# One load of a two-stage kernel (state-space scan, then gated feed-forward) moved from the head of block 1 to its middle

**Chip, cores, metric.** One core of a Trainium2 chip. The metric is device microseconds of one execution, lower is better; a profiled execution also gives its span (first to last instruction), some 1.8 us shorter than the time.

## The reference, cut to what matters

```python
# 4 sequences x 8 heads x 768 positions, 32 wide, state 16, float32
for each chunk of positions, in order:
    y      = (C B^T * decay mask) x  +  decayed (C state)
    state  = decay * state + decayed (B^T x)
# then, over 3072 tokens of 256 numbers (y with heads joined):
h   = y @ w_in            # 256 -> 2048
out = (h * cos(h)) @ w_out  # 2048 -> 256
```

## The kernel before

The kernel takes six chunks of 128 positions. Its main loop has 96 steps n, 16 to a block; block c = n // 16 runs the feed-forward of chunk c while the scan of chunk c + 1 is woven in. A step has a first matmul (`hp`), an activation over ScalarE, VectorE and ScalarE again (`k`, `w`, cos in place, `gT`) and, two steps later, a second matmul (`o`). All loads below are issued by one engine, SyncE (`nc.sync`), in program order. A chunk's B, C and x lie in one of two sets of buffers, so chunk 3 takes chunk 1's. From the second half of chunk 2 on, B and C for the transposed path come as 32 small "block" loads of 8 KB each, four to a step. The row loads (`arow`, 512 KB) and along loads (`along`, 64 KB) bring the decay factors of the scan.

```python
loads = ctx.enter_context(tc.tile_pool(name="loads", bufs=2))
...
def load(c, seqs=(0, NB)):                     # chunk c: B, (C,) x into tiles bc and xr
    ...
        raw[c] = (loads.tile([P, 2, NB * H, N], FP32, tag="bc", name="bc"),
                  loads.tile([P, NB, H, D], FP32, tag="xr", name="xr"))
    ...
    for dst, src in ((bc[:, 0, rs], B), (bc[:, 1, rs], C), (xr[:, rs], x))[::2 if c > 2 else 1]:
        nc.sync.dma_start(out=dst, in_=src[...])
...
def load_blocks(c, u):                         # 32 loads of [32, 4, 16] each
    ...
                    nc.sync.dma_start(out=to_[:, k, s, m, h], in_=of[m, h])
                    yield
...
def turn_blocks(c, u): ...                     # VectorE transposes: turned <- blocks
def turn2(c, u): ...                           # ScalarE: cT <- turned;  VectorE: rT
def intra2(c, u): ...                          # TensorE: g = cT x turned
def finish2(c, us): ...                        # TensorE: y, and s_ps, the last reader of x
...
halves_of = {2: [(2, 0, 0), (3, 0, 1), (5, 1, 0), (6, 1, 1), (7, 2, 0), (8, 2, 1), (10, 3, 0),
                 (11, 3, 1)]}                  # step in the block, sequence, half: VectorE's scans
...
block_loads = {NF * (c - 1) - 9 + 8 * u: (c, u) for c in range(2, NC) for u in range(2)
               if by_blocks(c, u)}             # chunk 2, half 1: steps 15 to 22

rest_of_loads()
for n in range(NC * NF + LAG):
    c, f = divmod(n, NF)                       # NF = 16
    if n < NC * NF:
        if f == 0 and c > 0:
            load(c + 2)
        first(n)
    ...
    # chunk 1's second half: finish2 at step 21
    # chunk 2's second half: turn_blocks at the end of step 26, turn2 in step 27, intra2 in step 28
    for at, (c, u) in block_loads.items():
        ...
            for _ in range(4):
                next(loading)
```

## Time and profile before

| | kernel before |
|---|---|
| time, median of its three runs | 383.96 us (383.78 to 384.23) |
| span of the profiled execution | 381.8 us |
| TensorE busy | 371.9 us, 97% |
| granted TensorE clock, mean | 0.989 |
| step 24 to step 40 (hp start to hp start) | 65.51 us |
| step 40 to step 56 | 58.74 us |

TensorE sets the time, so a pause of another engine costs only where TensorE runs out of work. The two last rows are the way to find such a place in a loop: equal pieces of work should take equal time. They, the hole between them and the chain of waits that leads to it are shown line by line in the prediction. In a line of a timeline the first number is the start, the second the time until the end of the group, and the bracket gives the idle time just before it and what ended that. A line with `<-` between two engines, such as `SPq L119 <- PE s_ps L509: 13.8, 1, 13.8`, is a wait: total us, times, longest. PE is TensorE, PEld its weight loads, DVE VectorE, ACT ScalarE, POOL GpSimd and SPq the queue of SyncE. The granted clock is the share of full speed that TensorE was given; "half clock" is 0.5.

### The profile page before, as it was taken

The page shows a single profiled execution, that of the slowest core. Times are in us where ns is not written, and L with a number is a line of the kernel's source. Part 1 is how long each engine was busy: PE and PEld are TensorE (multiplying, and loading weights), DVE is VectorE, ACT ScalarE, POOL GpSimd, SP SyncE. Part 2 cuts the span into 40 slices and gives each one's busy share as a digit, 9 for nine tenths or more (in the row PEclk, how much of TensorE's full clock was granted, in tenths as well). Part 3 has the DMA queues.
Part 4 walks back from the last instruction along what each step waited for, and adds up shares of the span by engine and source line. Part 5 has one row for each costly group of instructions (what it writes and reads, how often), then busy time and mean ns, then how long its engine had stood idle before and what let it go on. Part 6 is the DMA issues. An engine that isn't in the chain of part 4 may idle for free.

```text
span 381.8 us, 7915 instructions
## 1 busy us (share of the span) xinstructions
PE 371.9 (97%) x2952; PEld 328.6 (86%) x2952; DVE 278.5 (73%) x436; ACT 176.2 (46%) x305; POOL 213.7 (56%) x330
## 2 busy tenths in 40 slices
PE   8999999999999599999999999999999999999996
PEld 2578888888999499998989998989998989999995
DVE  8879999799687546987766887865888772554543
ACT  3887756444343233444433444443444443434441
POOL 6767564579764344694353775354666443444551
PEclk9999999999999699999999999999999999999999
DMA  6989889923544442944215843121020010010011
GB/s 81 258 230 290 250 218 131 164 59 29 78 112 98 106 107 21 136 116 114 46 22 61 146 96 80 22 39 18 4 40 8 2 27 2 2 28 2 2 27 27
DMA packets 123606, 31.48 MB, mean 82 GB/s; under 512 B 92753, under 2 KB 119473, under 8 KB 123569
## 3 DMA queue, kind: packets, MB, share of 16 engines
q1 hardware_dynamic: 123408, 30.86, 40.1%
q8 instruction: 23, 0.38, 0.4%
q10 hardware_dynamic: 160, 0.13, 0.1%
q14 instruction: 15, 0.11, 0.1%
HBM read 27.64 MB, written 3.34 MB: 81 GB/s over the span
## 4 chain that ended last, share of the span: by engine, by line
PE 93%; DVE 3%; POOL 1%; SPq 1%; DMA 1%; issue 1%; ACT 0%; DVEq 0%; POOLq 0%; ACTq 0%
PE hp L550 42%; PE o L647 31%; PE o L609 7%; PE g L454 3%; PE y L488 3%; PE y L481 1%; PE warm L101 1%; PE a_ps L317 1%; DVE mag L227 1%; PE g L392 1%; POOL w_in L235 1%; DMA blocks<-in_C_dram 1%; PE o L692 0%; PE s_ps L509 0%; DVE sum L664 0%
## 5 line engine op out<-in xcount | busy, mean ns | idle before, releaser
L550 PE MATMUL hp<-yT,w_in 128*128 128x256 f32 x768 | 185.5, 385 | 0.5 <-POOL w_in L235 0.3
L550 PEld LDWEIGHTS hp<-yT,w_in 128*128 128x128 f32 x768 | 140.5, 192 | 22.1 <-issue 3.5
L591 POOL TENSOR_TENSOR gd<-gT 128x256 f32<-128x256 f32 x79 | 59.9, 758 | 102.2 <-DVE gT L566 84.0
L561 ACT ACTIVATE w<-w,quarter 128x512 f32<-128x512 f32 x96 | 69.2, 721 | 73.6 <-DVE w L556 73.6
L556 DVE SCALAR_TENSOR_TENSOR w<-hp,k 128x512 f32<-128x512 f32 x96 | 65.5, 682 | 48.5 <-ACT k L554 48.2
L554 ACT ACTIVATE k<-hp 128x512 int32<-128x512 f32 x96 | 57.2, 595 | 89.3 <-PE hp L550 89.1
L566 DVE TENSOR_TENSOR gT<-hp,w 128x512 f32<-128x512 f32 x96 | 65.1, 678 | 34.3 <-ACT w L561 29.1
L647 PE MATMUL o<-words,gd 128*128 128x128 f32 x474 | 65.9, 275 | 0.0
L647 PEld LDWEIGHTS o<-words,gd 128*128 128x128 f32 x474 | 59.3, 192 | 0.0
L363 DVE TENSOR_TENSOR_SCAN lam<-arow,unit 128x512 f32<-128x512 f32 x40 | 55.8, 1395 | 0.0
L647 PEld LDWEIGHTS o<-w_out,gT 128*128 128x128 f32 x316 | 47.6, 191 | 4.1
L594 POOL TENSOR_TENSOR gd<-gT,gd 128x128 f32<-128x128 f32 x79 | 47.2, 598 | 6.2
L647 PE MATMUL o<-w_out,gT 128*128 128x128 f32 x316 | 48.0, 274 | 0.0
L593 POOL TENSOR_TENSOR gd<-gT,gd 128x128 f32<-128x128 f32 x79 | 42.4, 537 | 6.2
L609 PE MATMUL o<-w_out,gT 128*128 128x256 f32 x128 | 30.3, 380 | 0.4 <-POOL w_out L235 0.4
L647 PE MATMUL o<-words,gT 128*128 128x128 f32 x158 | 30.6, 275 | 0.0
L647 PE MATMUL o<-w_out,gd 128*128 128x128 f32 x158 | 30.5, 275 | 0.0
L609 PEld LDWEIGHTS o<-w_out,gT 128*128 128x128 f32 x128 | 24.2, 190 | 4.0 <-POOL w_out L235 0.8
L467 DVE TENSOR_TENSOR m<-g,lam 128x512 f32<-128x512 f32 x40 | 25.5, 679 | 0.0
L647 PEld LDWEIGHTS o<-words,gT 128*128 128x128 f32 x158 | 24.0, 192 | 0.0
L647 PEld LDWEIGHTS o<-w_out,gd 128*128 128x128 f32 x158 | 24.0, 192 | 0.0
L346 POOL TENSOR_TENSOR sc<-bc,lam 128x128 f32<-128x128 f32 x20 | 8.3, 417 | 16.7 <-DVE lam L363 9.4
(96 smaller groups left out, 286.0 us busy)
## 6 DMA issues: line engine op xcount, KB each, us to landing
arow<-a_cut SPq DMA_DIRECT2D x20, 512.0 KB
words<-in_moe_w_in_dram SPq DMA_DIRECT2D x8, 512.0 KB
words<-in_moe_w_out_dram SPq DMA_DIRECT2D x8, 512.0 KB
out_dram<-sum SPq DMA_DIRECT2D x18, 128.0 KB
xr<-in_x_dram SPq DMA_DIRECT2D x4, 512.0 KB
blocks<-in_B_dram SPq DMA_DIRECT2D x112, 8.0 KB
blocks<-in_C_dram SPq DMA_DIRECT2D x112, 8.0 KB
along<-a_all SPq DMA_DIRECT2D x20, 64.0 KB
```

The costliest lines, as they stand in the source:

```text
L363: V.tensor_tensor_scan(out=lam[c, b][:, hs].rearrange("p h i -> p (h i)"), data0=rows_.rearrange("p h i -> p (h i)"), data1=unit.rearrange ...
L467: V.tensor_tensor(out=of[0], in0=g[q][:, :, s * 2 * P:(s + 1) * 2 * P], in1=of[1], op=ALU.mult)
L550: PE.matmul(to_[:, e], lhsT=w_in[:, k, fs], rhs=y[:, k, u], start=(k == 0), stop=(k == KT - 1), skip_group_check=True)
L554: ACT.activation(k, hp[n], AF.Copy, bias=0.25, scale=INV_2PI)
L556: V.scalar_tensor_tensor(out=w, in0=hp[n], scalar=INV_2PI, in1=k, op0=ALU.mult, op1=ALU.subtract)
L561: ACT.activation(cos, cos, AF.Sin, bias=quarter, scale=TWO_PI)
L566: V.tensor_tensor(out=gT[n], in0=hp.pop(n), in1=cos, op=ALU.mult)
L591: G.tensor_tensor(out=d[:, 0:2], in0=g[:, 1:2].to_broadcast([P, 2, P]), in1=g[:, 3::-3], op=ALU.subtract)
L593: G.tensor_tensor(out=d[:, 2], in0=g[:, 0], in1=d[:, 0], op=ALU.subtract)
L594: G.tensor_tensor(out=d[:, 3], in0=g[:, 2], in1=d[:, 2], op=ALU.subtract)
L609: PE.matmul(o[c, u][:, t], lhsT=g[:, 2 * e + t], rhs=w_out[:, 2 * j + e], start=(j == e == t == 0), stop=(j == NJ - 1 and e == 1), skip_gr ...
L647: PE.matmul(at[q], lhsT=a_[q], rhs=w[q], start=(j == 0 and q in starts), stop=(j == NJ - 1), skip_group_check=True)
```

## The change

The intent: chunk 3's B and x are asked for at step 16, though B's buffer comes free only after chunk 1's transposes at step 18 and x's only after chunk 1's last matmuls at step 21, and SyncE stands waiting meanwhile. Asked for at step 24, they find the buffers free.

```diff
         if n < NC * NF:
-            if f == 0 and c > 0:
+
+            if c > 0 and f == (NJ if c == 1 else 0):     # NJ = 8
                 load(c + 2)
             first(n)
```

## The prediction

> **What bounds the kernel now.** I read the page's head and its slices first, then a table of stretches, then the SyncE queue's own waits, then each engine around the one place where TensorE stands still. The loop runs over 96 steps n; block c holds steps 16c to 16c+15. A step is one first matmul (hp), one second (o, two steps behind) and the activation between them; the state-space scan of the next chunk is woven in.
>
> ```profile
> span 381.8 us, 7915 instructions
> PE 371.9 (97%) x2952; PEld 328.6 (86%) x2952; DVE 278.5 (73%) x436; ACT 176.2 (46%) x305; POOL 213.7 (56%) x330
> PE   8999999999999599999999999999999999999996
> PEclk9999999999999699999999999999999999999999
> ```
>
> TensorE is busy 97% and sets the time. In the loop there is one hole: slice 14 (124 to 134 us), where both its busy share and its granted clock drop. The next view cuts the span at hp starts that the chain of waits gives: 107.06 is step 24, 172.57 step 40, 231.31 step 56. The three rows are therefore 16 steps each, from the middle of one block to the middle of the next.
>
> ```profile
> core 0: us, PE busy (x) PEld busy (x) DVE busy (x) ACT busy (x) POOL busy (x), PEclk, DMA share, GB/s
> 107.06:172.57 65.51, 61.49 (x513) 55.83 (x513) 47.35 (x73) 24.10 (x40) 35.28 (x56) 0.95 0.53 104
> 172.57:231.31 58.74, 58.74 (x514) 54.10 (x513) 44.03 (x71) 25.29 (x42) 33.04 (x55) 1.00 0.43 75
> 231.31:290.05 58.74, 58.74 (x514) 54.10 (x513) 43.89 (x71) 25.29 (x42) 31.89 (x51) 1.00 0.18 33
> ```
>
> The matmul counts are the same within one record, the later two rows are 58.74 us and full, the first is 65.51. So 65.51 - 58.74 = 6.77 us is all that this stretch can give back. A finer table of the hole shows its two halves:
>
> ```profile
> 121.50:124.80 3.30, 3.28 (x22) 2.88 (x21) 1.51 (x5) 0.00 (x0) 0.38 (x1) 1.00 0.58 162
> 124.80:128.80 4.00, 0.00 (x1) 0.00 (x1) 1.45 (x4) 0.96 (x3) 0.00 (x0) 0.84 0.28 50
> 128.80:130.90 2.10, 2.10 (x17) 1.30 (x17) 2.10 (x3) 1.04 (x2) 0.75 (x2) 0.50 0.71 195
> 130.90:134.55 3.65, 3.65 (x10) 2.94 (x11) 2.00 (x4) 0.72 (x1) 2.93 (x6) 0.52 0.30 52
> ```
>
> TensorE stands for 4.0 us and then works for 5.75 us at half clock. What it waits for, from the timelines of the engines and of the queue:
>
> ```profile
> 128.80 2.09 PE L454 MATMUL g<-cT,turned 32*128 32x256 f32 x16 [4.02 <-ACT cT L443]
> 127.84 0.91 ACT L443 ACTIVATE cT<-turned,slot 128x256 f32<-128x256 f32 x2 [7.22 <-DVE turned L423]
> 127.36 0.45 DVE L423 STREAM_TRANSPOSE turned<-blocks 128x256 f32<-128x256 f32 x1 [4.34 <-DMA blocks<-in_C_dram]
> 123.55 2.32 SPq L137 DMA_DIRECT2D blocks<-in_C_dram  x4
> ```
>
> The matmul g of step 28 needs cT, cT needs the transposed block, and the block needs the last of 32 small loads, which the queue issued only at about 125.3 us. Why so late is in the queue's own waits and its timeline:
>
> ```profile
> SPq L119 <- PE s_ps L509: 13.8, 1, 13.8
> 85.61 0.38 SPq L119 DMA_DIRECT2D bc<-in_B_dram  x1
> 99.90 0.37 SPq L119 DMA_DIRECT2D xr<-in_x_dram  x1
> 103.75 2.37 SPq L137 DMA_DIRECT2D blocks<-in_B_dram  x4
> ```
>
> Chunk 3's B and x are asked for at step 16, but their buffer is chunk 1's, and chunk 1's last reader (s_ps, step 21) ends at 99.84 us. The x load waits 13.8 us at the head of SyncE's queue, and 28 of the 32 block loads of chunk 2, second half, stand behind it.
>
> **What the Trainium skill says.** "Perfetto Trace Analysis", section on the DMA instruction (HWDGE), has an issuing sequencer go through its semaphore wait first and be free for its next instruction only after the descriptors are made. The trace agrees: between 86.0 and 99.9 us SyncE issues nothing. "DMA: Bandwidth & Descriptors", Anatomy of one DMA, gives some 2.0 us of fixed cost to a transfer; the chain of waits here has 2.00 us from the last block load's issue to the transpose. "TensorE: Matmul & The Clock Gate", What's actually happening, says the array falls to half rate after an idle window of about 3.4 us and comes back after about 3.4 us of work. The trace agrees on halving after a 4.0 us gap (16 g matmuls take 2.09 us against 1.08 elsewhere) but shows 5.75 us of slow work; I use the measured one.
>
> **The change, part by part.** *Removed:* the load at step 16. Nothing then waits at the head of the queue for s_ps. *Added:* the same two loads at step 24, after chunk 1's buffer was freed at step 21. The number of transfers, bytes and compute instructions is unchanged, and so is the order on every engine but SyncE's queue.
>
> *Where the block loads then go.* From 99.9 to 125.87 us the queue works without a break; less the x issue (0.37) that is 25.6 us of issuing, for the stores, rows and block loads of steps 16 to 22. Without the wait it starts on them when step 14's output copy is there, about 82.6 us (81.91 + 0.67). Unhindered it would end at 82.6 + 25.6 = 108.2 us. It also has to wait for scans that free row buffers: the one of step 17 ends at 84.3, of step 19 at 91.95, of step 22 at 104.3 us. From the last: a row load (0.42), two along loads (1.3), four block loads (2.3) give 108.3 us. So the last block is issued at about 108.3 and lands at about 110.3. VectorE reaches the second transpose at 122.97 (122.60 plus the 0.37 that one takes of a pair). Slack about 12.5 us: the wait is gone with much to spare.
>
> *What then binds step 28.* The same place one block later (step 44) is the pattern: two transposes take 0.74 us, cT starts 0.03 later and takes 0.91, g starts 0.31 after the last group of o. Here that gives transposes done at 122.60 + 0.74 = 123.34, cT done at 124.28; TensorE gets to g at 124.39 + 0.31 = 124.70. In time by 0.4 us. Next, hp of step 29 needs the bank that gT of step 27 reads. On VectorE: w starts 123.27, rT 123.84, the scan 124.17 (1.21 us; step 43 has no such scan), gT 125.29 to 125.95. TensorE is done with g at 124.70 + 1.08 = 125.78. So about 0.2 us is left waiting, too short for a clock drop by what the trace shows (1 us pauses are not there to compare, so this is my choice).
>
> *The sum.* Idle 4.02, g at half clock 2.09 - 1.08 = 1.01, hp at half clock 3.67 - 1.92 = 1.75: together 6.78, the 6.77 of the table by another way. Less the new wait of 0.2: 6.55 us. **383.96 - 6.55 = 377.4 us.** Elsewhere nothing can come: the chain from step 18 to 28 and from 40 on is matmul behind matmul.
>
> **The rivals.** *A. The wait moves to another transfer.* The two loads are now in front of step 24's rows and blocks. The x issue before took 0.37 us, others of that kind up to 3.6 us, and the store behind x took 2.63, so the queue may lose some 6 us after 111 us. But what stands behind them are chunk 3's second-half rows, its blocks (first transposed at step 38, about 160 us) and the first store of sum. Chunk 3's B is first read past step 32 (about 140 us), so the loads have 30 us. I give this 6%; it would leave 2 to 4 us of the gain unseen, 379.5 to 381.5.
>
> *B. VectorE becomes the bound at steps 26 to 29.* With 4.3 us of its own idleness gone it has a scan, four sums, two reach scans and two transposes in a row. It is busy 12.08 of 14.44 us from 107 to 121.5. If my offsets are off by 0.5 us, g or hp waits up to 1 us: 377.5 to 378.5. About 20%.
>
> *C. The gain is larger than the hole.* It would need TensorE time to be lost elsewhere through the same wait; the pieces of steps 18 to 28 are 3.29 us each plus g, y, tp, with no gap. Under 5%, and only noise would bring it past 2%.
>
> *D. The blocks come late anyway,* because the scans or 64-byte packets hold them. 512 KB rows and 64 KB along loads share the engines with them; but the slack is 12.5 us. 2%, time unchanged.
>
> **Range and chances.** Two per cent faster means at most 376.3 us, 7.7 less, and the hole is 6.8. So the change should fall just short of that mark: faster 0.05. Slower needs a new stall of over 14 us, for which I see no candidate: 0.01. Within 2%: 0.94. The low end of the range is the whole hole plus a little noise (0.2 us between runs), 376.8; the high end leaves 1 us to rival B: 378.4.
>
> **What would show it.** Right: no SyncE wait for s_ps; x of chunk 3 issued near 111 us without a wait; the last block load of chunk 2 issued near 108 us and no DMA named before turned; slice 14 at 9 for TensorE and for its clock; the stretch from step 24 to step 40 at 58.7 to 59.2 us; mean clock near 1.0 from the 0.989 before; g at 1.08 us after at most some tenths of idle. A wait of hp for gT of 0.1 to 0.4 us in step 29 would confirm the small term. Wrong: a TensorE gap over 1 us between 108 and 170 us, above all behind chunk 3's blocks, rows or B; or transposes waiting for a DMA with the queue's issues in time (then it was transfer, not order).

## The result, and the profile after

Beside 384.10 us of the kernel before (four runs, 383.78 to 384.41), the changed kernel took 377.96 us (four runs, 377.46 to 378.32). The ratio of the two is 0.9839, with a 95% interval of 0.9822 to 0.9856. A ratio is the mean time of one kernel's fast runs over that of the other's fast runs of the same rounds, so not quite the ratio of the medians quoted. The gain of 6.1 us is within the 2% that is called the same, as forecast.

The page of the kernel after, its head and two rows of its slices:

```profile
span 376.5 us, 7915 instructions
PE 369.5 (98%) x2952; PEld 327.0 (87%) x2952; DVE 278.4 (74%) x436; ACT 176.1 (47%) x305; POOL 213.7 (57%) x330
PE   8989999999999999999999999999999999999996
PEclk9999999999999999999999999999999999999999
```

The instruction counts are those of before. The 5 in TensorE's row and the 6 in the clock's row are gone.

Stretches of the kernel after, cut like those of before (108.26 is its step 24, 167.29 step 40, 226.03 step 56), and three short ones through the place where the hole was (columns as in the prediction):

```profile
108.26:167.29 59.03, 58.78 (x514) 54.11 (x513) 47.16 (x73) 24.11 (x40) 35.30 (x56) 1.00 0.58 95
167.29:226.03 58.74, 58.74 (x514) 54.11 (x513) 44.04 (x71) 25.29 (x42) 33.04 (x55) 1.00 0.41 73
...
125.99:127.06 1.07, 1.07 (x16) 0.64 (x16) 1.07 (x2) 0.58 (x2) 0.40 (x1) 1.00 0.62 152
127.06:127.31 0.25, 0.00 (x1) 0.03 (x1) 0.25 (x2) 0.00 (x0) 0.01 (x2) 1.00 0.07 18
127.31:129.27 1.96, 1.96 (x10) 1.75 (x11) 1.10 (x3) 0.72 (x1) 1.63 (x3) 1.00 0.22 45
```

The stretch came down from 65.51 to 59.03 us, a gain of 6.48 us. The pause of 4 us became one of 0.25 us, and g and hp run at full clock. SyncE's queue in the kernel after, from the timeline:

```profile
107.25 2.32 SPq L137 DMA_DIRECT2D blocks<-in_C_dram  x4
109.61 2.28 SPq L137 DMA_DIRECT2D blocks<-in_B_dram  x4
111.99 0.41 SPq L119 DMA_DIRECT2D bc<-in_B_dram  x1
112.50 2.69 SPq L119 DMA_DIRECT2D xr<-in_x_dram  x1
115.28 3.45 SPq L145 DMA_DIRECT2D arow<-a_cut  x1
```

Chunk 2's last four block loads start to be issued at 107.25 us (123.55 before), and only then come the next chunk's first blocks and the two moved loads, without a wait; the list of the queue's waits no longer has s_ps at all. What VectorE and TensorE do with the blocks:

```profile
123.80 0.74 DVE L423 STREAM_TRANSPOSE turned<-blocks 128x256 f32<-128x256 f32 x2
125.91 1.15 PE L454 MATMUL g<-cT,turned 32*128 32x256 f32 x16
127.31 1.96 PE L550 MATMUL hp<-yT,w_in 128*128 128x256 f32 x8 [0.25 <-DVE gT L566]
```

Both transposes run back to back, g starts without a bracket, and the 0.25 us before hp are the small new wait for gT.

**The span tells another sum.** It fell by 5.3 us only (381.8 to 376.5), 1.2 us less than the stretch gave. The missing part lies at the start, in code that the change does not touch. One hp and the first o matmul of the kernel before, then of the kernel after:

```profile
23.22 1.97 PE L550 MATMUL hp<-yT,w_in 128*128 128x256 f32 x8 [0.15 <-DVE gT L566]
25.61 1.99 PE L609 MATMUL o<-w_out,gT 128*128 128x256 f32 x8 [0.42 <-POOL w_out L235]
```

```profile
24.43 1.97 PE L550 MATMUL hp<-yT,w_in 128*128 128x256 f32 x8 [1.06 <-DVE gT L566]
26.82 1.99 PE L609 MATMUL o<-w_out,gT 128*128 128x256 f32 x8 [0.42 <-POOL w_out L235]
```

The profiled execution of the kernel after is 1.21 us late at 26.8 us already. Leave the start out: 381.8 - 25.61 = 356.19 us and 376.5 - 26.82 = 349.68 us, a gain of 6.51. Whether the late start belongs to the change is the first question below.

### The profile page after: what moved, and what is told of

It reads as the page before. It is cut to its first block, busy times and chain, and to the rows that moved or that the text cites. A ratio compares the mean times of both kernels' runs of the same rounds, so it can differ in the third digit from the quotient of the medians.

```text
span 376.5 us, 7915 instructions
## 1 busy us (share of the span) xinstructions
PE 369.5 (98%) x2952; PEld 327.0 (87%) x2952; DVE 278.4 (74%) x436; ACT 176.1 (47%) x305; POOL 213.7 (57%) x330
## 4 chain that ended last, share of the span: by engine, by line
PE 89%; SPq 4%; DMA 3%; DVE 2%; issue 1%; ACT 1%; POOL 0%; ACTq 0%; DVEq 0%; POOLq 0%
PE hp L550 42%; PE o L647 31%; PE o L609 7%; SPq L119 3%; PE g L454 3%; PE y L488 3%; DMA words<-in_moe_w_in_dram 2%; PE y L481 1%; DMA blocks<-in_B_dram 1%; PE o L692 1%; PE s_ps L509 0%; SPq L186 0%; DVE gT L566 0%; PE tp L437 0%; POOL w_out L235 0%
## 5 line engine op out<-in xcount | busy, mean ns | idle before, releaser
L664 DVE TENSOR_TENSOR sum<-ps,sum 128x256 f32<-128x256 f32 (+1 forms) x27 | 16.7, 644 | 0.6
```

## The experiments

Three accounts of the gain were open. **Queue order:** the x load waits for s_ps at the head of SyncE's queue, and the block loads behind it come late; the wait itself costs nothing. **Contention:** the 768 KB of B and x crowd the DMA engines just when the blocks are due, and it helps to have them out of the way. **The clock:** how much of the loss was idle time, and how much the half clock after it.

All results in one table. "Rest" is the span of the profiled execution less the start of its first o matmul, so free of the start; "stretch" is g of step 24 to g of step 40, sixteen steps. Times are medians; each ratio is against the kernel before on the same chip.

| run | time (runs) | ratio | first o | rest | stretch |
|---|---|---|---|---|---|
| kernel before | 383.96 (3) | 1 | 25.61 | 356.19 | 65.51 |
| kernel after | 377.96 (4) | 0.9839 | 26.82 | 349.68 | 59.03 |
| after_again | 377.41 (5) | 0.9823 | 25.90 | 349.70 | 59.04 |
| after_third | 377.50 (5) | 0.9826 | 26.57 | 349.73 | 59.04 |
| x_alone_late | 377.09 (4) | 0.9820 | 25.64 | 349.76 | 59.03 |
| b_alone_late | 384.43 (4) | 1.0001 | 26.05 | 356.45 | 65.77 |
| blocks_first | 378.03 (4) | 0.9833 | 26.40 | 349.70 | 59.03 |
| third_buffer | 378.10 (4) | 0.9848 | 26.59 | 349.71 | 59.02 |
| step18 | 377.14 (4) | 0.9831 | 25.59 | 349.71 | 59.04 |
| step17 | 382.57 (4) | 0.9945 | 26.91 | 354.39 | 63.74 |
| step17_again | 381.08 (4) | 0.9922 | 25.91 | 353.29 | 62.61 |
| row_first | 378.20 (4) | 0.9844 | 26.65 | 349.75 | 59.06 |
| filled_hole | 381.90 (4) | 0.9947 | 25.92 | 354.18 | 63.50 |
| scan_later | 377.29 (4) | 0.9828 | 26.19 | 349.41 | 58.77 |

The first o matmul started anywhere from 25.59 to 26.91 us, in kernels that do not differ before that point (third_buffer aside, which makes one table in place). The rest, by contrast, is the same within 0.1 us wherever the hole is closed (349.68 to 349.76), but for scan_later, which changes one thing more and has 349.41.

### The changed kernel twice more

The edit is none.

> The changed kernel once more, for its size and for the question why its first profile lay 1.2 us late before the hole was even reached. Theory (queue order): the stretch from step 24 to step 40 takes 59.0 us as in the first profile (65.51 before, 58.74 in steady state), time 377.5 to 378.2. If the late start (first o matmul at 26.82 us against 25.61) is scatter from run to run, it lies between 25.5 and 27 here, and differs from 26.82; if it belongs to the change, it is 26.8 again and again later than that of the kernel before.

> The changed kernel as the partner of the one with the later scan, on the same chip: stretch 59.0; first o matmul somewhere from 25.5 to 27 us, as the prologue falls out.

As expected: stretch 59.04 in both; the first o at 25.90 and 26.57 us in place of 26.82. So the late start is scatter from run to run, not a cost of the change. The medians, 377.41 and 377.50 us, are also a little under that of the first four runs.

### Which of the two loads counts

The edit, shortened (the code has slices for `B`, `x` and `both`):

```diff
+            # x_alone_late: B stays at step 16; b_alone_late: x stays there
-            if f == 0 and c > 0:
-                load(c + 2)
+            if f == 0 and c > 0:
+                load(c + 2, only=B if c == 1 else both)      # or: only=x
+            if c == 1 and f == NJ:
+                load(3, only=x)                              # or: only=B
```

> Only the x load is moved to step 24, B stays at step 16. Theory: x alone waits for s_ps (13.8 us), B waits only for the transposes of step 18 (3.5 us), so the whole gain comes from x: 377.5 to 378.3, stretch from step 24 to 40 at 59.0. Rival contention (it is the 768 KB out of the way of the block loads that helps, 256 KB of it B): part of the gain is missing, 379 to 381. Rival that both count: near 381.

> The counterpart: only B is moved, x stays at step 16 and waits for s_ps there. Theory: no gain, the hole is as before, 383.6 to 384.4, stretch from step 24 to 40 at 65 to 66 us and a SyncE wait for s_ps of some 14 to 17 us. Rival contention: a third of the bytes is gone from in front of the blocks, about 382.

x alone brings all of the gain and B alone none. The queue's waits with B alone moved, and the g matmul that follows from them:

```profile
SPq L120 <- PE s_ps L510: 18.1, 1, 18.1
...
129.44 2.09 PE L455 MATMUL g<-cT,turned 32*128 32x256 f32 x16 [4.22 <-ACT cT L444]
```

The wait for s_ps is even longer, 18.1 us in place of 13.8, since x now reaches the head of the queue without the B load's own wait before it; the hole stays as it was. With 256 KB out of the way of the blocks nothing was gained, which speaks against contention.

### The wait kept, but with nothing urgent behind it

```diff
-    block_loads = {NF * (c - 1) - 9 + 8 * u: (c, u) for ...
+    block_loads = {NF * (c - 1) - 9 + 8 * u - 8 * ((c, u) == (2, 1)): (c, u) for ...
```

> The load of B and x stays at step 16 as in the kernel before and still waits for s_ps, but the 32 block loads of chunk 2, second half, are put before it (steps 7 to 14 in place of 15 to 22). Theory: the wait is still there, 13 us or so, and costs nothing, because nothing that is due soon stands behind it: 377.5 to 378.3, stretch at 59.0. Rival (the wait itself costs, or what else stands behind it: stores, rows, along loads): a good part of the 6 us is still lost, 381 to 384.

The load is at step 16 as in the kernel before. The queue in this run, its waits and its timeline:

```profile
SPq L119 <- PE s_ps L509: 10.0, 1, 10.0
...
84.86 4.62 SPq L137 DMA_DIRECT2D blocks<-in_C_dram  x8
90.10 0.52 SPq L119 DMA_DIRECT2D bc<-in_B_dram  x1
100.69 0.37 SPq L119 DMA_DIRECT2D xr<-in_x_dram  x1
```

x waits for s_ps for 10 us (I had put down some 13), the stores, rows and along loads stand behind it, and the gain is there in full (rest 349.70). The wait itself costs nothing; the block loads behind it did.

### The early load kept, but without a wait

```diff
-                      loads.tile([P, NB, H, D], FP32, tag="xr", name="xr"))
+                      loads.tile([P, NB, H, D], FP32, tag="xr", name="xr", bufs=3))
-    la = const.tile([RB, NU, P], FP32, name="la")
+    la = a_in                                   # room for the third buffer
```

> The load stays at step 16, but x has three buffers, so chunk 3's x need not wait for chunk 1's (one small table is made in place to have the room; that is no work more or less). Theory: no wait for s_ps, blocks issued in time though B and x move at the old time among them: 377.5 to 378.3, stretch from step 24 to 40 at 59.0. Rival contention: 512 KB of x and 256 KB of B move just when the blocks do, blocks late, 380 to 384.

x in this run, from the queue's timeline:

```profile
87.01 2.09 SPq L119 DMA_DIRECT2D xr<-in_x_dram  x1
```

B is issued at 86.59 and x at 87.01 us, and stores and the block loads of steps 16 to 22 come right behind them. The rest is 349.71 us. So 768 KB in front of the blocks cost nothing once the queue doesn't wait: contention is refuted as the cause. The median of this run is at the slow end of the group; in its profiled execution the first o was late (26.59).

### How early may the load be?

```diff
-            if c > 0 and f == (NJ if c == 1 else 0):
+            if c > 0 and f == (1 if c == 1 else 0):      # step17; step18: 2
```

> The load of the change put at step 17 in place of 24: x still waits until 100 us or so, but the stores and four block loads of step 16 are in front of it. In the kernel before these took 3.33 and 2.37 us of queue time after x, some 2 us of it back-pressure of x that would fall on the next issue. Theory: the last block load is issued 3.5 to 5.7 us earlier than before, at 120 to 122.5, lands at 122 to 124.5, VectorE wants it at 123: g waits between 0 and 1.2 us, with no clock drop to speak of. 377.7 to 379.5, that is most of the gain for one step. Rival (any wait at the head of the queue costs its length): 383.

> The load at step 18, wait for s_ps still over 10 us. Theory: four more block loads, a row, two stores and two along loads are in front (5.4 us), so the last block lands by 120 and nothing waits for it: as the change, 377.5 to 378.3, stretch at 59.0, although the load waits at the head of the queue nearly as long. Rival: 382 to 383.

At step 18 the load waited 7.2 us for s_ps, less than the 10 us that I had put down, and nothing was lost. At step 17 my expectation failed: 382.57 us, with three runs at 382.2 to 383.1 and one at 379.33. The queue's timeline of step17 shows why the block loads gained so little:

```profile
101.20 0.37 SPq L119 DMA_DIRECT2D xr<-in_x_dram  x1
101.66 2.46 SPq L145 DMA_DIRECT2D arow<-a_cut  x1
104.21 2.98 SPq L617 DMA_DIRECT2D out_dram<-ob  x2
...
113.79 5.68 SPq L137 DMA_DIRECT2D blocks<-in_B_dram  x8
```

From x's issue at 101.20 to the last block load's end at 125.97 us the queue took 24.8 us, against 26.0 in the kernel before (99.90 to 125.87): 1.2 us won, where I had counted on 3.5 to 5.7. I had allowed for x holding up the next issue (2.46 us for a row load that takes 0.42 otherwise), but not for that row load, 512 KB itself, holding up the stores after it (2.98 us for two against 1.36). A further 1.05 us went to eight block loads (5.68 against 4.63). They stand 12 us later, behind another row load, as they do in the kernel before, so the first row load does not explain them; why they were slower was not tested. Two more runs were to test that.

```diff
+            # row_first: after the scan of step 17 and its row load, in place of before them
+            if n == NF + 1:
+                load(3)
```

> The load at step 17 once more, because my expectation of it missed by 4 us and its four times lay in two places (three near 382.7, one at 379.3). Reading of the first profile: x and the 512 KB of rows now follow one another in the queue, the DMA engines are full for 6 us behind them, and SyncE's later issues take longer (two stores 2.98 us against 1.36, eight block loads 5.68 against 4.63), so the last block was issued only 1.2 us earlier than before; at the edge, some executions still lose the clock. Expected: again times in both places or near 382.6, with the last block load issued at 124.5 to 126 us where it is slow and by some 123 where it is fast.

> The load at step 17 too, but behind that step's row load in place of in front of it. Reading (back-pressure of two large transfers in a row): what is left behind x takes 20.6 us of queue time by the durations of the kernel before (stores 3.33, along loads 1.30, blocks 4.63, row 0.42, blocks 4.63 and 2.28, row 0.42, along 1.25, blocks 2.32), so the last block is issued by about 121 after the x at 100.4 and lands at 123, the moment it is wanted: g waits at most some tenths, no clock drop, 377.2 to 378.5, stretch from step 24 to 40 at 59.0 to 59.6. Rival (step 17 was slow for a reason other than the order of rows and x): near 382.6 as before.

With the row load ahead of x, all is well: the last block load ends at 122.44 us, 21.5 us after x was issued, and g does not wait. So the order of x and that row load decides it, but the reason is shown only in part. The two stores, now right behind x, took 3.30 us (2.98 in step17, 3.33 in the kernel before): they are held up as much as ever. The 3.3 us won against step17 are the row's own 2.46 us, now in front of x, and the 1.0 us of the eight block loads, which took 4.64. The repetition of step17 was of the slow kind throughout, 381.0 to 381.6, and its last block load ended at 123.85 us, a little before the 124.5 that I had given for slow runs. The one run at 379.33 was not profiled and was not seen again. Its mean clock is 0.999, as in runs without the hole, where the other three have 0.991 to 0.996. So it lost little or nothing to the half clock, which is part of its lead; why, and the rest of it, stay open.

Two lines of that repetition bear on the clock:

```profile
126.79 1.15 PE L454 MATMUL g<-cT,turned 32*128 32x256 f32 x16 [1.71 <-ACT cT L443]
128.56 3.39 PE L550 MATMUL hp<-yT,w_in 128*128 128x256 f32 x8 [0.63 <-DVE gT L566]
```

hp ran at half clock here: 3.39 us against 1.97. Cut into pieces of 0.02 us, the trace has the granted clock fall at 128.03 us, when the second pause was only 0.1 us old, and come back at 131.44. So a pause of 1.71 us and 1.15 us of work had been enough. The half clock lasted 3.41 us, in step17 as well (130.15 to 133.57), and twice that, 6.82 us, in the kernel before (127.55 to 134.37) and in b_alone_late (128.31 to 135.13). In these four profiles it comes in steps of 3.4 us and begins during a pause. That suggests that the cost of a pause depends on where in such a step it falls; no run tested this.

### How much was the clock?

```diff
         g = [pair("g") for _ in range(2)]
+        if (c, u) == (2, 1):
+            fill(g[0][:, 0].rearrange("p (k i) -> p k i", k=4), 4)
```

> The kernel before, with four matmuls on the table of ones (some 3.4 us at full clock) into g's bank, overwritten at once, just ahead of the g matmuls that wait in the hole. The blocks are as late as before. Theory: the wait stays (g at about 4 us after o), but TensorE does not fall to half clock, so g takes 1.08 and hp 1.9 us again: 2.76 us of the 6.8 come back, 381.0 to 381.6, stretch at 62.7. Rival (the slow g and hp have another cause than the idle time, such as VectorE being busy): 383.5 to 384.5.

This is the kernel before with the hole filled by four matmuls (eight records in the trace) whose result is overwritten at once:

```profile
124.93 3.60 PE L101 MATMUL g<-ones 128*128 128x512 f32 x8
129.11 1.15 PE L456 MATMUL g<-cT,turned 32*128 32x256 f32 x16 [0.59 <-ACT cT L443]
130.89 1.97 PE L552 MATMUL hp<-yT,w_in 128*128 128x256 f32 x8 [0.63 <-DVE gT L568]
```

g starts as late as before (129.11 - 25.92 = 103.19 us after the first o, before 128.80 - 25.61 = 103.19), but g and hp run at full clock, and 2.0 us come back. I had 2.76, and the time is 0.3 us above my range. Most of the difference is a wait of hp for gT of 0.63 us that the slow g had hidden. So of the hole's 6.8 us some 4.1 were waiting for the blocks, 2.0 is what the half clock cost by itself, and some 0.7 is that wait of hp, of which 0.25 is left in the kernel after.

### The last quarter of a microsecond

```diff
-                     (11, 3, 1)]
+                     (12, 3, 1)]        # VectorE's last half scan of chunk 2: step 28 for 27
```

> The change, and VectorE's last half scan of chunk 2 moved from step 27 to step 28, where gT waits for GpSimd anyway. Theory for the last 0.25 us: hp of step 29 waits for gT of step 27 only because of this 1.21 us scan, so the wait goes (gT ends about 1 us earlier) and the stretch from step 24 to 40 comes to 58.74 to 58.8 in place of 59.0. In the time that is 0.2 to 0.3 us of 378, less than the scatter between runs, so the profile decides. Rival (the wait is some other lag, or the scan then delays hp of step 30): stretch 59.0 or more.

From the timelines of this run, TensorE's g and hp and VectorE's gT between them:

```profile
125.28 1.15 PE L454 MATMUL g<-cT,turned 32*128 32x256 f32 x16
126.41 1.97 PE L550 MATMUL hp<-yT,w_in 128*128 128x256 f32 x8
...
125.57 0.69 DVE L566 TENSOR_TENSOR gT<-hp,w 128x512 f32<-128x512 f32 x1 [0.75 <-ACT w L561]
```

gT ends before g does, hp follows g without a wait, and the stretch is 58.77 us, the steady state's 58.74 but for 0.03. In the time, 377.29 against 377.50 us on the same chip, this can't be told from scatter; only the profile shows it. It is the best version of the series by its rest (349.41 us).

## Why the prediction was right

The time forecast was 377.4 us; measured were 377.96, 377.41 and 377.50, all within the range of 376.8 to 378.4. With the scatter of the start described below, a median so near the forecast is partly luck; the stretch is the better test, 59.03 us against 58.74 + 0.2 = 58.94 forecast.

- **The hole and its size.** The table of stretches gave 6.77 us as all there was; 6.48 of them came back (65.51 to 59.03). The split was less exact: the forecast put 2.76 us down to the half clock, and filled_hole gave 2.0 of them back. Nor was the half clock 5.75 us long: the granted clock was 0.5 for 6.82 us, from 127.55 on, and only some 5.6 us of that fell on work. The sum does not use that figure.
- **Its cause.** Shown, not only argued: with x alone moved all of the gain is there, with B alone none; with the wait kept but the blocks in front, all; with a third buffer and the load where it was, all.
- **The block loads' new place.** Forecast: the last issued by about 108.3 us. It ended at 109.57 in an execution that started 1.21 us late, so 108.36 on the clock of the kernel before.
- **The new small wait.** Forecast 0.2 us for gT, from the offsets of the same place one block later. It was 0.25 in the first profile and 0.25 to 0.28 in the other runs without the hole, and it went with the scan that I had named (scan_later). My choice, that so short a pause costs no clock, held.
- **Rival A,** a wait moved to other transfers: the queue did lose time behind the moved loads, as I had it (x 2.69 and the row load behind it 3.45 us, where unhindered ones take some 0.4), but no TensorE gap followed.
- **Rival B,** VectorE as the bound: only those 0.25 us.
- **What I had not seen.** I put the scatter between runs at 0.2 us. The changed kernel's runs spread over 1.4 us (376.92 to 378.32). First o matmuls at 25.90 to 26.82 us in its three profiles account for much of it. In the late profile ScalarE waited 0.94 us for a piece of w_in in the prologue, and the first four `a_ps` matmuls there took 1.36 us in place of 1.08.

## What to carry to other kernels

A load that must wait for its buffer holds up everything that the same engine issues after it, so put it where the buffer is already free, or put the loads that are due sooner in front of it; the wait as such cost nothing here (blocks_first, step18). To find and size such a loss, compare equal pieces of the loop in a table of stretches, and count the half clock that follows a pause with the pause. Then ask what comes second in line at that spot: here it was a 1.21 us scan and worth 0.25 us. When counting queue time, add what a large load does to the issues after it.

## What the Trainium skill lacked or had wrong

- "TensorE: Matmul & The Clock Gate", What's actually happening: it gives a free-running window of about 3.4 us, and the half rate after an idle one. The length is borne out: half clock for 3.41 us in step17_again and twice that, 6.82 us, in the kernel before. But the window was not idle: in the 3.41 us before the clock fell, TensorE had worked some 1.6 us in step17_again (and 0.65 in the kernel before). Pauses of 0.59 and 0.63 us in filled_hole brought no fall.
- "DMA: Bandwidth & Descriptors", Issuing engines are not separate DMA queues: it calls the sequencer's time to initiate a DMA usually small relative to the DMA itself. It gives no number for small loads, and for the 8 KB block loads the issue set the pace: four take 2.3 us, so the 28 behind the waiting x took some 16 us of queue time, and between 119 and 121 us, where they are issued one behind the other, the DMA engines were busy only 0.16 of the time.
- "Perfetto Trace Analysis", DMA Instruction — HWDGE: it has no number for how long a large load holds up later issues of the same engine. Here a row load took 2.46 to 3.45 us right behind a 512 KB x load, and mostly 0.42 elsewhere.
